# A fused Fourier layer and token FFN on one Trainium2 core: small products on the second stage's PSUM banks at planned places, the inverse second stage two steps later, C stored by quads, half of the threshold off VectorE

## Chip, core and metric

The kernel runs on one core of a Trainium2 chip. The metric is the device time in microseconds (us) of one execution. The kernel before takes 909.07 us, the median of 2 runs (907.66 to 910.48).

## The reference, cut to what matters

Eight batches of 3136 rows and 256 columns go through a real FFT along the rows, a complex 256x256 product per frequency, a bias, a soft threshold and the inverse FFT. Then 128 rows of each batch, those with the largest score, go through a small FFN and are written back.

```python
X = np.fft.rfft(x, axis=1)                      # x: 8 x 3136 x 256
Yr = Xr @ w_r - Xi @ w_i + b_r
Yi = Xr @ w_i + Xi @ w_r + b_i
Yr = np.sign(Yr) * np.maximum(np.abs(Yr) - lam, 0.0)   # the same for Yi
y = np.fft.irfft(Y, n=x.shape[1], axis=1)
...
scores = np.einsum('bsd,d->bs', y, w_gate)
top_idx = np.argpartition(-scores[b], capacity)[:capacity]   # capacity 128
h = np.maximum(xe @ w1, 0.0)
ye = h @ w2
out[b, top_idx] = y[b, top_idx] + g[:, None] * ye     # g = sigmoid(score)
```

## The kernel before

The FFT of 3136 points is done in two stages, 98 x 32, both as products with cosine and sine tables on TensorE (PE).

- **First stage** (`s1`, inverse `s1i`). A piece is 4 of the 32 columns n2 of a batch, so a batch has 8 pieces. GpSimd (POOL) forms sum and difference of the two halves (`uv_x`, lines 409 and 410; `uv_c`, lines 575 and 576; VectorE does the forward pair of batch 0 and the inverse difference of the last batch). Four products per piece go to two PSUM banks, ScalarE (ACT) copies them out (line 432 into `at`, line 584 into `ot`), and a DMA stores them: forward to the DRAM scratch `As`, inverse to the output.
- **Second stage, forward** (`s2`). A quad is a sixth of a batch's frequencies. It is loaded from `As` (tile `av`, two steps ahead), 32 small products fill the two banks of `px`, ACT casts `px` to the high part `Xh` (line 462) and VectorE (DVE) forms the low part `Xl` (line 463). `s2t` does the two odd frequencies of a batch in a bank of `s`.
- **Spectral product** (`spectral`). Per quad two halves p = 0 and 1, each 12 products of 512 columns (high x high, high x low, low x high) into one bank of `py`. `shrink` then does the threshold: DVE adds the bias in PSUM (line 479), ACT forms relu(z - 2 lam) into `r` (line 481), DVE forms min(z, 0) + r into `Y` (line 482). `spectral_t` does it for the odd frequencies.
- **Second stage, inverse** (`s2i`). 16 products into four banks of `s`. ACT copies each bank into `ct` (line 527), DVE forms the bank's part of the scores (`score_part`, line 509, name `junk`). Four DMAs per quad store `ct` into the DRAM scratch `Cs`, and `ld_c` loads a quarter of `Cs` as `cin` with one DMA.
- **Routing and FFN.** `score` transposes the score parts of a batch (`Csc`), multiplies them by `wq` and has the scores. `select` finds the 128th largest by a search over the bits of the float: per level DVE compares and counts (`f`, `c`, `n`, lines 269, 272, 277), PE sums the counts over partitions (`s<-n,tm`), DVE takes the digit (`ok`, `d`, `w`, lines 291 to 294). `place` turns the threshold into row numbers, `gather` fetches the rows, `prepare`, `hidden` and `combine` are the FFN. Batches 0 to 3 are selected together with 2 bits a level (16 levels), 4 and 5 together, 6 and 7 alone with 3 bits.

PSUM has 8 banks: `px` 2, `py` 2, and `s` 4. Everything but the forward second stage and the spectral products takes its bank from the ring `s`: both first stages, `s2i`, `s2t`, `s2it`, and every small product of routing and FFN.

The order of the work is written by hand. A step t is one quad; 48 steps make the main loop. In a step: all planned `s1` and `s1i` pieces (lists `F1` and `I1`), a turn of the routing threads, `s2` of quad t+1, `s2i` of quad t-1, the load of `av` for t+2, sums and differences, `spectral` half 0 with one turn of the threads in its middle, half 1 with another, then loads of `cin`. In steps 2 to 10 `consts_moe` loads a slice of the FFN weights and ACT rounds it (line 243). Threads are Python generators: a turn runs each one to its next `yield`, whatever the engines are doing. The engines execute their own instructions in the order in which the program issues them. All plain DMAs are issued by SyncE (SP, line 203). The matmuls all have line 206.

After the loop come the eight `s1i` pieces of batch 7, with one turn of the threads per piece, and then the rest of the routing and the FFN.

Of the kernel before, what the change touches and what calls it, by code (L numbers as in the profile page):

```python
# [20 lines left out]
N1, N2 = 98, 32  # L21
# [35 lines left out]
def _tables():  # L57
# [52 lines left out]
    gi = gi.reshape(6, 2, 128, 2, 2, 2, 16).transpose(2, 0, 1, 3, 5, 4, 6).reshape(128, NJ, 64)  # L110
# [3 lines left out]
    git = np.zeros((64, 2, 2, 16))  # L114
    for m, (r, k) in enumerate(fr):
# [45 lines left out]
def fourier_moe(ctx: ExitStack, tc: tile.TileContext, x, w_r, w_i, b_r, b_i, wg, w1, w2,  # L161
# [14 lines left out]
    second = c_tile([128, 2, NJ, 64], F32, "second")  # L176
# [19 lines left out]
    XB, CB = 3, 2  # L196
# [21 lines left out]
    def consts_w():  # L218
        for z, src in enumerate((w_r, w_i)):
# [3 lines left out]
            nc.vector.tensor_copy(h, t)  # L223
            nc.vector.tensor_tensor(out=l, in0=t, in1=h.bitcast(F32), op=ALU.subtract)
# [3 lines left out]
    def consts_bias():  # L228
# [24 lines left out]


    def select(bs, bits, thrs):
# [7 lines left out]
        for hi, i in zip([32] + cuts, cuts):  # L263
            m = 2 ** (hi - i) - 1
            f = pool.tile([N1, nb, m], U32, name="f" + tag, bufs=1)
            if w is None:
                nc.vector.memset(f, 0)
            else:
                nc.vector.tensor_tensor(out=f, in0=digits[:, 8 * i:8 * i + m].rearrange("p (o m) -> p o m", o=1).broadcast_to([N1, nb, m]),  # L269
                                        in1=w.broadcast_to([N1, nb, m]), op=ALU.bitwise_xor)  # L270
            c = pool.tile([N1, nb, m, N2], BF16, name="c_6" if nb == 1 else "c" + tag, bufs=1)
            nc.vector.tensor_tensor(out=c, in0=sv.broadcast_to([N1, nb, m, N2]),  # L272
# [3 lines left out]
            with nc.allow_low_precision(reason="counts up to 32 are exact"):  # L276
                nc.vector.tensor_reduce(out=n, in_=c, axis=AX.X, op=ALU.add)  # L277
            yield
            yield
            tot = ps.tile([N1, nb, m], F32, name="s", bufs=4)  # L280
            mm(tot, ones, n)
            w2 = pool.tile([N1, nb, 1], U32, name="w" + tag)
            if w is None:
                nc.vector.tensor_scalar(out=w2.bitcast(I32), in0=tot, scalar1=cap - 0.5, scalar2=1.0, op0=ALU.is_ge, op1=ALU.subtract)
            else:
                d = pool.tile([N1, nb, 1], U32, name="d" + tag, bufs=1)
                if m == 1:
                    nc.vector.tensor_scalar(out=d, in0=tot, scalar1=cap - 0.5, scalar2=None, op0=ALU.is_ge)
                else:
                    ok = pool.tile([N1, nb, m], F32, name="ok" + tag, bufs=1)  # L290
                    nc.vector.tensor_scalar(out=ok, in0=tot, scalar1=cap - 0.5, scalar2=None, op0=ALU.is_ge)  # L291
                    with nc.allow_low_precision(reason="whole numbers"):
                        nc.vector.tensor_reduce(out=d, in_=ok, axis=AX.X, op=ALU.add)  # L293
                nc.vector.scalar_tensor_tensor(out=w2, in0=d, scalar=i, in1=w, op0=ALU.logical_shift_left, op1=ALU.bitwise_xor)  # L294
# [4 lines left out]
    def place(b, thr, slots):  # L299
        m = pool.tile([N1, 2, N2], BF16, name="mask")  # L300
        nc.vector.tensor_scalar(out=m[:, 0, :], in0=scores[:, b, :], scalar1=thr, scalar2=None, op0=ALU.is_gt)
        nc.vector.tensor_scalar(out=m[:, 1, :], in0=scores[:, b, :], scalar1=thr, scalar2=None, op0=ALU.is_equal)
        mf = m.rearrange("p a c -> p (a c)")
        yield
        yield
        pt = ps.tile([2 * N2, N1], F32, name="s", bufs=4)
        mm(pt, mf, eye)
        mt = pool.tile([2 * N2, N1], BF16, name="mt")
        nc.vector.tensor_copy(mt, pt)
        yield  # L310
        yield
        pp = ps.tile([N1, 2, N2], F32, name="s", bufs=4)
        mm(pp.rearrange("p a c -> p (a c)"), mt, upper[:2 * N2, :])
        row = pool.tile([N1, 2, N2 + 2], F32, name="row")
        nc.vector.tensor_copy(row[:, :, :N2], pp)
        cnt = pool.tile([N1, 2], BF16, name="cnt")
        nc.vector.tensor_copy(cnt, pp[:, :, N2 - 1])
        for a in range(2):
            nc.vector.tensor_copy(row[:, a, N2 + 1:], nrow)
        yield  # L320
        yield
        pb = ps.tile([N1, 2], F32, name="s", bufs=4)
        mm(pb, lower, cnt, True, False)
        mm(pb[:, 1:2], ones, cnt[:, 0:1], False, True)
        nc.vector.tensor_copy(row[:, :, N2], pb)
        end = pool.tile([N1, 2], F32, name="end")
        nc.vector.tensor_tensor(out=end, in0=row[:, :, N2], in1=row[:, :, N2 - 1], op=ALU.add)  # L327
        for k in range(NCHK):
            n = min(128, cap - 128 * k)
            hot = pool.tile([N1, 2, n], F32, name="hot", bufs=1)  # L330
            io = iota[:N1, 128 * k:128 * k + n]
            for a in range(2):
                nc.vector.tensor_scalar(out=hot[:, a, :], in0=io, scalar1=row[:, a, N2:N2 + 1], scalar2=None, op0=ALU.is_ge)
                nc.vector.scalar_tensor_tensor(out=hot[:, a, :], in0=io, scalar=end[:, a:a + 1], in1=hot[:, a, :],  # L334
                                               op0=ALU.is_lt, op1=ALU.mult)
            yield
            yield
            pi = ps.tile([n, N2 + 2], F32, name="s", bufs=4)
# [3 lines left out]
            nc.vector.tensor_tensor(out=r, in0=tcol[:n, k:k + 1], in1=pi[:, N2:N2 + 1], op=ALU.subtract)  # L342
            le = pool.tile([n, N2], F32, name="le")
            c = pool.tile([n, 1], F32, name="col")
            nc.vector.tensor_scalar(out=le, in0=pi[:, :N2], scalar1=r, scalar2=None, op0=ALU.is_le)
            nc.vector.tensor_reduce(out=c, in_=le, axis=AX.X, op=ALU.add)
            idx = idxs[:n, NCHK * b + k:NCHK * b + k + 1]
            nc.vector.tensor_tensor(out=idx, in0=c, in1=pi[:, N2 + 1:], op=ALU.add)
# [460 lines left out]
```

## Time and profile before

| what | us |
|---|---|
| median of the runs | 909.07 |
| the profiled execution | 909.2 |
| its span, first to last instruction | 907.4 |
| around the span | 1.8 |
| first forward second stage (first step) starts at | 51.7 |
| that of the last quad starts at | 741.3 |
| last inverse second stage ends at | 786.7 |

Times in the rows are microseconds from the start of the span unless marked ns. A PE row's duration is modelled and overlaps with the next one's, so the pace of matmuls is read from their starts. "PEld" is PE's weight load. What stands behind "<-" is what ended an engine's idle time.

### The profile page before, as it was taken

To read this page: it belongs to the slowest core of one execution; us is meant where nothing else is said; L and a number is where in the kernel's file an instruction comes from. 1 tells how busy PE (TensorE), PEld (TensorE's weight loads), DVE (VectorE), ACT (ScalarE), POOL (GpSimd) and SP (SyncE) were. 2 spreads that over 40 slices of the span, in tenths; PEclk is the share of its full clock that TensorE was granted. 3 is DMA by queue.
4 is the path that set the end of the run, shared out by engine and by line. 5 is a ranking of instruction groups with operands and counts; after the bars stand their busy time and mean duration, and the time that the engine had idled before them with its cause. 6 is when DMAs were issued, how large, how long until landed. Compare 5 with 4: busy or idle time off the path is not lost. (4 is left out here: it accounts for less than half of the span.)

```text
span 907.4 us, 19138 instructions
## 1 busy us (share of the span) xinstructions
PE 723.9 (80%) x7618; PEld 476.0 (52%) x7618; DVE 444.8 (49%) x1244; ACT 333.1 (37%) x654; POOL 314.5 (35%) x266
## 2 busy tenths in 40 slices
PE   3369787767899899888797889898898978658775
PEld 1046555445666566555454555566566655422565
DVE  5225443332454354447655654655667765414652
ACT  2235243343455535553443444344233232202110
POOL 0233232436265536535441634344222132022101
PEclk9579898887999999998989999999899897855677
DMA  5787655766698779878765867675545433343100
GB/s 179 223 253 235 212 162 163 219 180 193 176 269 249 255 214 293 260 210 244 209 194 167 228 192 225 195 205 162 155 124 153 130 109 112 87 144 107 53 7 18
DMA packets 86995, 162.53 MB, mean 179 GB/s; under 512 B 8221, under 2 KB 60794, under 8 KB 86906
## 3 DMA queue, kind: packets, MB, share of 16 engines
q1 hardware_dynamic: 86010, 159.14, 59.8%
q0 software_dynamic: 896, 2.17, 0.8%
q8 instruction: 60, 0.98, 0.5%
q14 instruction: 29, 0.24, 0.1%
HBM read 83.22 MB, written 78.12 MB: 178 GB/s over the span
## 5 line engine op out<-in xcount | busy, mean ns | idle before, releaser
L206 PE MATMUL py<-wh,Xh 128*128 128x512 f32 x384 | 171.3, 446 | 2.4 <-issue 2.4
L481 ACT ACTIVATE r<-py,m2l 128x512 f32<-128x512 f32 (+1 forms) x104 | 69.8, 671 | 261.8 <-DVE py L479 259.7
L206 PE MATMUL py<-wl,Xh 128*128 128x512 f32 x384 | 159.1, 414 | 2.9 <-issue 2.9
L206 PE MATMUL py<-wh,Xl 128*128 128x512 f32 x384 | 159.8, 416 | 1.0 <-issue 1.0
L575 POOL TENSOR_TENSOR cu<-cin 113x512 f32<-113x512 f32 x64 | 82.1, 1283 | 190.1 <-DMA cin<-Cs 122.7
L463 DVE TENSOR_TENSOR Xl<-px,Xh 128x1024 fp32r<-128x1024 f32 x48 | 58.8, 1224 | 160.2 <-ACT Xh L462 160.1
L409 POOL TENSOR_TENSOR xu<-xt 113x512 f32<-113x512 f32 x56 | 71.9, 1284 | 173.2 <-PE s L206 172.3
L206 PE MATMUL s<-cu,first 49*64 49x512 f32 (+1 forms) x256 | 98.3, 692 | 37.9 <-POOL cu L575 16.9
L206 PE MATMUL s<-Y,second 32*64 32x256 f32 x1536 | 93.5, 449 | 42.2 <-DVE XTl L474 16.1
L509 DVE CUSTOM_DVE_ANT_0 junk<-s,wgb 128x256 f32<-128x256 f32 (+1 forms) x200 | 84.5, 422 | 44.8 <-PE s L206 21.7
L482 DVE SCALAR_TENSOR_TENSOR Y<-py,r 128x512 f32<-128x512 f32 x96 | 66.3, 691 | 78.3 <-ACT r L481 78.3
L527 ACT COPY ct<-s 128x256 f32<-128x256 f32 x192 | 66.8, 374 | 101.9 <-DVE Csc L509 61.7
L206 PEld LDWEIGHTS py<-wh,Xh 128*128 128x128 f32 x384 | 78.1, 203 | 47.7 <-issue 31.9
L206 PE MATMUL s<-xu,first 64*64 64x512 f32 (+1 forms) x256 | 73.1, 661 | 25.9 <-DVE xu L409 14.9
L206 PE MATMUL s<-cv,first 64*64 64x512 f32 (+1 forms) x256 | 87.9, 696 | 3.1 <-DVE cv L576 3.1
L479 DVE TENSOR_TENSOR py<-py,bias 128x512 f32<-128x512 f32 x96 | 66.7, 695 | 48.0 <-PE py L206 47.6
L206 PEld LDWEIGHTS py<-wl,Xh 128*128 128x128 f32 x384 | 77.4, 202 | 22.2 <-issue 3.3
L206 PEld LDWEIGHTS py<-wh,Xl 128*128 128x128 f32 x384 | 78.5, 205 | 17.2 <-issue 3.2
L584 ACT COPY ot<-s 113x512 f32<-113x512 f32 x128 | 67.9, 608 | 50.7 <-issue 28.7
L206 PEld LDWEIGHTS s<-Y,second 32*64 32x64 f32 x1536 | 43.3, 149 | 71.8 <-ACT ot L584 22.8
L206 PEld LDWEIGHTS px<-second,av 64*64 64x64 f32 x3072 | 62.6, 143 | 31.0 <-issue 14.8
L432 ACT COPY at<-s 113x512 f32<-113x512 f32 x128 | 66.0, 595 | 23.6 <-PE s L206 21.6
(109 smaller groups left out, 959.2 us busy)
## 6 DMA issues: line engine op xcount, KB each, us to landing
xt<-in_x SPq DMA_DIRECT2D x64, 392.0 KB
As<-at SPq DMA_DIRECT2D x64, 392.0 KB
cin<-Cs SPq DMA_DIRECT2D x32, 784.0 KB
out<-ot SPq DMA_DIRECT2D x64, 392.0 KB
av<-As SPq DMA_DIRECT2D x48, 512.0 KB
Cs<-ct SPq DMA_DIRECT2D x192, 128.0 KB
second<-t_second SPq DMA_DIRECT2D x2, 768.0 KB
w1s<-in_moe_w SPq DMA_DIRECT2D x1, 1024.0 KB
```

The costliest lines, as they stand in the source:

```text
L206: return nc.tensor.matmul(out, a, b, start=start, stop=stop)
L409: e.tensor_tensor(out=u, in0=t[:, 0, :], in1=t[:, 1, :], op=ALU.add)
L432: nc.scalar.copy(out=tv[:, r, :], in_=banks[r][:PT])
L463: nc.vector.tensor_tensor(out=lv, in0=p, in1=hv.bitcast(F32), op=ALU.subtract)
L479: nc.vector.tensor_tensor(out=p, in0=p, in1=bs, op=ALU.add)
L481: nc.scalar.activation(out=r1, in_=p, func=AF.Relu, bias=m2l[:p.shape[0]], scale=1.0)
L482: nc.vector.scalar_tensor_tensor(out=y, in0=p, scalar=0.0, in1=r1, op0=ALU.min, op1=ALU.add)
L509: nc.vector.tensor_tensor_reduce(out=junk[:r], in0=p, in1=wgb[:r], scale=1.0, scalar=0.0, op0=ALU.mult, op1=ALU.add, accum_out=Csc[b][:r, ...
L527: nc.scalar.copy(out=t[:, k], in_=banks[k])
L575: e.tensor_tensor(out=u, in0=t[:, 0, :], in1=t[:, 1, :], op=ALU.add)
L584: nc.scalar.copy(out=tv[:, r, :], in_=banks[r][:PT])
```

## The change

1. **Banks.** `px` becomes two tiles of one bank, `px0` and `px1`. The forward second stage fills both and empties each by itself. Every small product of routing and FFN, and the odd rows of the inverse (`s2it`), take them in turn (`m_tile`); `s2t` takes a `py` bank. Only `s1`, `s1i` and `s2i` are left in `s`.
2. **Places by running estimates.** Each matmul and each DVE instruction adds an estimate to a running clock of its engine while the program is written out. A thread yields the delay that it wants after its last DVE work, and a turn runs it only when PE's clock has reached that point. Turns are offered after every 3 spectral products (four in half 0, three in half 1).
3. **Later inverse.** `s2i` of quad t-2 instead of t-1 stands in step t; `s1i` begins at step 9 of a batch instead of 8.
4. **Threshold.** In half 1 DVE adds the bias into SBUF (`r0`); ACT then forms relu(z - 2 lam) and relu(-z), POOL subtracts the two. These three stand in the next step, behind `s2i`'s copies. Half 0 and the odd rows stay as they were.
5. **First-stage pieces.** One piece stands at the start of a step and the others between the two spectral halves.
6. **C.** `Cs` is laid out by quads: one store of 512 KB instead of four of 128 KB. A load of `cin` becomes three DMAs (48, 48 and 2 partitions).
7. **Rest.** Four buffers for `xt` (three before), three for `ct` (two); loads of `xt` ahead of the stores; the selection groups are (0,1), (2,3), (4,5), 6, 7; the score parts are issued in turns.

```diff
     def mm(out, a, b, start=True, stop=True):
+        k, m, n = b.shape[0], out.shape[0], int(np.prod(b.shape[1:]))
+        part = 8 if k <= 32 else 4 if k <= 64 and m <= 64 else 1
+        if part != clk["part"]:
+            clk["part"], clk["PE"] = part, clk["PE"] + 0.15
+        clk["PE"] += max(n * (1.68 if b.dtype == F32 else 0.45), 220 if b.dtype == F32 else 110) / part / 1000
         return nc.tensor.matmul(out, a, b, start=start, stop=stop)
+    class Vector:
...
+                clk["V"] = max(clk["V"], clk["PE"] + 0.2) + VB + n * VN
+                return f(*args, **kw)
+    def m_tile(shape):
+        turn[0] ^= 1
+        return ps.tile(shape, F32, name=f"px{turn[0]}", bufs=1)
...
-            yield
-            yield
-            tot = ps.tile([N1, nb, m], F32, name="s", bufs=4)
+            yield SL
+            tot = m_tile([N1, nb, m])
...
-        p = ps.tile([128, 2, 8, 64], F32, name="px", bufs=1)
+        p = [ps.tile([128, 8, 64], F32, name=f"px{kap}", bufs=1) for kap in range(2)]
...
-        nc.scalar.copy(out=hv, in_=p)
-        nc.vector.tensor_tensor(out=lv, in0=p, in1=hv.bitcast(F32), op=ALU.subtract)
+            for kap in range(2):
+                nc.scalar.copy(out=hv[:, kap], in_=p[kap])
+                vec.tensor_tensor(out=lv[:, kap], in0=p[kap], in1=hv[:, kap].bitcast(F32), op=ALU.subtract)
...
-        p = ps.tile([128, 2, 97], F32, name="s", bufs=4)
+        p = ps.tile([128, 2, 97], F32, name="py", bufs=2)
...
-        nc.vector.tensor_tensor(out=p, in0=p, in1=bs, op=ALU.add)
+        q = p if eng is vec else pool.tile(list(p.shape), F32, name="r0", bufs=2)
+        vec.tensor_tensor(out=q, in0=p, in1=bs, op=ALU.add)
...
+            def rest():
+                nc.scalar.activation(out=r1, in_=q, func=AF.Relu, bias=m2l[:p.shape[0]], scale=1.0)
+                nc.scalar.activation(out=q, in_=q, func=AF.Relu, scale=-1.0)
+                eng.tensor_tensor(out=y, in0=r1, in1=q, op=ALU.subtract)
+            shrinks.append(rest)
...
-        def store():
-            for p in range(2):
-                for half in range(2):
...
+        later.append(lambda: ld(Cs[b][0][g].rearrange("k p d -> p k d"), t))
...
-        ld(t[P0:], Cs[b][:, :, :, 4 * i:4 * i + 4, :].rearrange("p a r n d -> (a r) p n d"))
+        for a in range(2):
+            ld(t[16 + 48 * a:64 + 48 * a], c[a, :, :, 4 * i:4 * i + 4, :])
+        ld(t[P0::97], Cs[b][1].rearrange("(q a n) d -> a q n d", q=2, a=2)[:, :, 4 * i:4 * i + 4, :])
...
+    MID0, MID1, SL, FG, SC = (0, 1, 2, 3), (0, 1, 2), 0.15, 6.0, 4
-    I1 = [2, 3, 3, 4, 5, 5, 6, 6]
+    F1, I1 = [-2, -1, 0, 1, 1, 2, 3, 3], [9, 10, 10, 11, 12, 12, 13, 14]
...
+    def tick(most=None, wait=False):
+        score_some(SC)
+        most = MOST if most is None else most
+        for t in sorted(threads, key=lambda t: t[1]):
+            if most and (t[1] <= clk["PE"] or wait):
...
+            firsts = [(s1, a) for a in todo(t, "s1")] + [(s1i, a) for a in todo(t, "s1i")]
+            for f, a in firsts[:NQ]:
+                f(*a)
...
+                forward(t + 1)
+            inverse.append(t)
+            if t == T - 1:
+                flush(shrinks)
+            while inverse and inverse[0] <= t - (LAG if t < T - 1 else 1):
+                backward(inverse.pop(0))
+            flush(later)
+            flush(shrinks)
...
+            spectral(b, g, 0, tick)
+            last_rows()
...
+            for f, a in firsts[NQ:]:
+                f(*a)
...
+            spectral(b, g, 1, tick)
```

Three places show how it moves the instructions.

ACT in one step of the main loop, before: the two `r` are the threshold of the step's two halves, `at` and `ot` are the first-stage pieces of the next step, `Xh` and `ct` its second stages.

```order
L481 ACTIVATE r_3780<-py,m2l 128x512
L481 ACTIVATE r_3807<-py,m2l 128x512
L432 COPY at<-s 113x512 x4
L584 COPY ot<-s 113x512 x4
L462 CAST Xh<-px 128x2x8x64
L527 COPY ct<-s 128x256 x4
```

ACT in one step now (line numbers of the changed file):

```order
L461 COPY at<-s 113x512 x2
L502 CAST Xh<-px_3522 128x8x64
L502 CAST Xh<-px_3523 128x8x64
L584 COPY ct<-s 128x256 x4
L528 ACTIVATE r_3506<-r_3504,m2l 128x512
L529 ACTIVATE r_3504<-r_3504 128x512
L524 ACTIVATE r_3639<-py,m2l 128x512
L633 COPY ot<-s 113x512 x2
```

The threshold of half 1 (the pair of lines 528 and 529) has moved behind the next step's copies and reads SBUF; only one `r` per step still reads a `py` bank in the step itself.

PE in half 0 of a step with selection, before: `py` is the spectral product, `n` the counts of one level.

```order
L206 MATMUL s<-Y,second 64x256 x16
L206 MATMUL py<-wh,Xh 128x512
L206 MATMUL py<-wh,Xl 128x512
L206 MATMUL py<-wl,Xh 128x512
L206 MATMUL py<-wh,Xh 128x512
L206 MATMUL py<-wh,Xl 128x512
L206 MATMUL py<-wl,Xh 128x512
L206 LDWEIGHTS tm
L206 MATMUL s<-n_4676,tm 98x12
```

PE in half 1 of such a step now:

```order
L216 MATMUL s<-cu,first 64x512
L216 MATMUL s<-cv,first 64x512
L216 MATMUL py<-wh,Xh 128x512
L216 MATMUL py<-wh,Xl 128x512
L216 MATMUL py<-wl,Xh 128x512
L216 LDWEIGHTS tm
L216 MATMUL px_3289<-n_3237,tm 98x6
L216 MATMUL py<-wh,Xh 128x512
```

The small product stands behind 3 spectral products instead of 6, writes a `px` bank, and has a first-stage piece in front of the half.

DVE behind the last inverse second stage, before: `Csc` is the last score part of batch 7, `cv` the difference of a loaded piece, `ok` to `n` one level of selection, `sct` the score transpose.

```order
L509 ISA junk,Csc<-s,wgb 64x256
L509 ISA Csc 64x1
L576 TENSOR_TENSOR cv<-cin_90 113x512
L291 TENSOR_SCALAR ok_8713<-s 98x7
L293 TENSOR_REDUCE d_8712<-ok_8713 98x1
L294 SCALAR_TENSOR_TENSOR w_8711<-d_8712,w_8555 98x1
L269 TENSOR_TENSOR f_8717<-digits,w_8711 98x7
L272 TENSOR_TENSOR c_8719<-scores,f_8717 98x224
L277 TENSOR_REDUCE n_8721<-c_8719 98x7
L576 TENSOR_TENSOR cv<-cin_90 113x512
L309 CAST mt<-s 64x98
L556 COPY sct<-s 25x128
```

The same place now, with two row searches (`row`, `end`, `hot`) between what is shown and `sct`:

```order
L230 ISA Csc 128x1
L230 TENSOR_TENSOR cv<-cin_91 113x512 x2
L230 TENSOR_SCALAR ok_9045<-px_9041 98x7
L230 TENSOR_REDUCE d_9044<-ok_9045 98x1
L230 SCALAR_TENSOR_TENSOR w_9043<-d_9044,w_8922 98x1
L230 TENSOR_TENSOR f_9049<-digits,w_9043 98x7
L230 TENSOR_TENSOR c_9051<-scores,f_9049 98x224
L230 TENSOR_REDUCE n_9053<-c_9051 98x7
L230 COPY row<-px_9055 98x2
L230 TENSOR_TENSOR end<-row 98x2
```

Both differences still stand ahead of the selection and of `sct`, but the transpose and the score product are now in PE's order ahead of all eight pieces of batch 7, not among them.

## Rows read from the trace of the kernel before

**Rows 1.** The page's first part: busy us, share of the span, instructions.

```profile
PE 723.9 (80%) x7618; PEld 476.0 (52%) x7618; DVE 444.8 (49%) x1244; ACT 333.1 (37%) x654; POOL 314.5 (35%) x266
```

**Rows 2.** Windows: length, busy us per engine, granted clock, DMA share, GB/s, by stage.

```profile
0.00:51.70 51.70, 15.89 (x68) 4.85 (x68) 19.12 (x28) 12.10 (x21) 5.12 (x8) 0.73 0.63 200
51.70:741.30 689.60, 593.32 (x6878) 396.14 (x6882) 352.51 (x960) 291.15 (x571) 280.49 (x234) 0.93 0.70 203
741.30:786.70 45.40, 37.81 (x311) 23.72 (x304) 26.89 (x84) 15.03 (x32) 10.23 (x9) 0.85 0.30 86
786.70:907.40 120.70, 76.93 (x370) 51.28 (x368) 46.32 (x173) 14.81 (x30) 18.70 (x16) 0.65 0.23 68
```

**Rows 3.** Waits in the main loop, 51.7 to 741.3: us in total, times, longest.

```profile
ACT r L481 <- DVE py L479: 238.4, 97, 5.4
...
PE s L206 <- ACT at L432: 36.1, 26, 6.0
...
ACT w2h L243 <- DMA xe<-in_moe_w: 26.3, 8, 5.5
...
PE s L206 <- ACT ct L527: 18.6, 17, 2.1
```

**Rows 4.** Timeline at 464 to 466 us, ACT, then PE: start, us, what, idle before.

```profile
464.65 0.69 ACT L481 ACTIVATE r<-py,m2l 128x512 f32<-128x512 f32 x1 [3.28 <-DVE py L479]
465.24 2.04 ACT L432 COPY at<-s 113x512 f32<-113x512 f32 x4
465.96 0.61 PE L206 MATMUL s<-cu,first 64*64 64x512 f32 x1 [1.74 <-ACT at L432]
```

**Rows 5.** Timeline of PE at 405 to 409 us, one step without a wait.

```profile
405.84 1.16 PE L206 MATMUL px<-second,av 64*64 64x64 f32 x64
406.94 1.12 PE L206 MATMUL s<-Y,second 32*64 32x256 f32 x32
407.99 0.50 PE L206 MATMUL py<-wh,Xh 128*128 128x512 f32 x1
408.32 0.39 PE L206 MATMUL py<-wh,Xl 128*128 128x512 f32 x1
408.55 0.39 PE L206 MATMUL py<-wl,Xh 128*128 128x512 f32 x1
```

**Rows 6.** Groups by line over the span: busy us, mean ns, idle before.

```profile
L481 ACT ACTIVATE r<-py,m2l 128x512 f32<-128x512 f32 (+1 forms) x104 | 69.8, 671 | 261.8 <-DVE py L479 259.7 <-DMA xt<-in_x 2.1
L482 DVE SCALAR_TENSOR_TENSOR Y<-py,r 128x512 f32<-128x512 f32 x96 | 66.3, 691 | 78.3 <-ACT r L481 78.3
...
L410 POOL TENSOR_TENSOR xv<-xt 113x512 f32<-113x512 f32 x56 | 72.1, 1288 | 0.0
L509 DVE CUSTOM_DVE_ANT_0 junk<-s,wgb 128x256 f32<-128x256 f32 (+1 forms) x200 | 84.5, 422 | 44.8 <-PE s L206 21.7 <-ACT ct L527 1.6 <-ACT ctt L543 0.2
```

**Rows 7.** One selection level on DVE in the timeline at 772 us, first and last of six.

```profile
772.01 0.16 DVE L291 TENSOR_SCALAR ok<-s 98x7 f32<-98x7 f32 x1
...
773.22 0.39 DVE L277 TENSOR_REDUCE n<-c 98x7 bf16<-98x224 bf16 x1
```

**Rows 8.** Tile `mask` on DVE: duration ns min/median/max.

```profile
L301 DVE TENSOR_SCALAR mask<-scores,w x8: 232/241/2997, 544.7 to 877.4; 98x32 bf16<-98x32 f32 x8
```

**Rows 9.** Timeline behind the loop: SP, DVE and PE.

```profile
792.45 0.79 SPq L203 DMA_DIRECT2D cin<-Cs  x2
798.77 0.69 DVE L576 TENSOR_TENSOR cv<-cin 113x512 f32<-113x512 f32 x1 [10.49 <-DMA cin<-Cs]
807.21 0.41 PE L554 MATMUL s<-ident,Csc 128*25 128x128 f32 x1
823.15 1.20 PE L206 MATMUL s<-sct,wq 25*98 25x32 f32 x6
882.39 0.23 PE L206 MATMUL s<-tm,mask 98*64 98x98 bf16 x1
```

**Rows 10.** Window of the densest stretch, columns as in rows 2.

```profile
335.00:438.00 103.00, 91.75 (x1145) 59.95 (x1151) 52.40 (x126) 50.46 (x101) 54.37 (x44) 0.97 0.83 248
```

More of the change, by code (lines that the diff above doesn't have):

```diff
@@ L413, in uv_x @@
         if n < 8 * B:
-            later.append(lambda: ld_x(*divmod(n, 8)))
+            loads.append(lambda: ld_x(*divmod(n, 8)))
     def quarters(z, uv):
@@ L423, in quarters, with evict @@
         return banks
+    count = [0]
+    def evict(tv, banks):
+        count[0] += 1
+        for r in range(2):
+            if r == 1 and count[0] % EV[1] < EV[0]:
+                vec.tensor_copy(tv[:, r, :], banks[r][:PT])
+            else:
+                nc.scalar.copy(out=tv[:, r, :], in_=banks[r][:PT])
     def s1(b, i):
@@ L430, in s1 @@
         tv = t.rearrange("p (r c) d -> p r (c d)", r=2)
-        for r in range(2):
-            nc.scalar.copy(out=tv[:, r, :], in_=banks[r][:PT])
+        evict(tv, banks)
         later.append(lambda: ld(As[b][:, 4 * i:4 * i + 4, :], t[P0:]))
@@ L685, in quad, with forward, backward, last_rows @@
         return divmod(t, Q)
+    loads, inverse, tails = [], [], []
+    def forward(n):
+        b, g = quad(n)
+        s2(b, g)
+        if g == Q - 1:
+            s2t(b)
+    def backward(n):
+        score_some(9)
+        b, g = quad(n)
+        s2i(b, g)
+        if g == Q - 1:
+            tails.append(b)
+    def last_rows():
+        if tails:
+            s2it(tails[0])
+            score_some(9)
+            done["s2i"] = tails.pop()
+            flush(later)
+    def load_a(n):
+        b, g = quad(n)
+        ld_a(b, g)
+        if g == Q - 1:
+            ld_at(b)
+    def sums(t):
+        for f, what, made, n in ((uv_x, "uvx", xuv, 2), (uv_c, "uvc", cuv, 2)):
+            for s in (t - 1, t):
+                while todo(s, what) and len(made) < n:
+                    a = todo(s, what)[0]
+                    f(*a)
+                    plan[s].remove((what, a))
     with tc.manual_schedule():
         for t in xts + cts:
-            nc.vector.memset(t[:P0].rearrange("p a c -> p (a c)") if len(t.shape) == 3 else t[:P0].rearrange("p a c d -> p (a c d)"), 0.0)
+            vec.memset(t[:P0].rearrange("p a c -> p (a c)") if len(t.shape) == 3 else t[:P0].rearrange("p a c d -> p (a c d)"), 0.0)
         ld(first.rearrange("p z c s -> p (z c s)"), t_first)
@@ new lines, in fourier_moe @@
+        sums(-1)
+        flush(loads)
+        forward(0)
+        ld(sec[:, 1].rearrange("p j s -> p (j s)"), t_second[:, NJ * 64:])
+        for t in range(T):
+            if t + 2 < T:
+                load_a(t + 2)
+            for a in todo(t, "ldc"):
+                ld_c(*a)
+            flush(loads)
+            firsts = [(s1, a) for a in todo(t, "s1")] + [(s1i, a) for a in todo(t, "s1i")]
+            for f, a in firsts[:NQ]:
+                f(*a)
+                sums(t - 1)
+            score_some(9)
+            if t + 1 < T:
+                forward(t + 1)
[4 more added lines that the diff above has]
+                backward(inverse.pop(0))
+            flush(later)
+            flush(shrinks)
@@ L754, in fourier_moe @@
-            tick(threads)
-            spectral(b, g, 1, mid)
+                sums(t - 1)
+            flush(later)
+            sums(t)
+            spectral(b, g, 1, tick)
             X.pop((b, g))
```

385 lines of the change are left out of this document (190 added, 195 removed).

## Prediction

> **What bounds the kernel now.** I read the page's busy shares first, then the span cut into stages, then what ended the waits in the longest stage, then the timeline at one such wait.
>
> TensorE is busy 80% of the span [rows 1]; ACT, DVE and POOL are far from full. The reader is to see that no engine is a bound by itself and that the order of the work costs the rest. By stage [rows 2]: 51.7 us until the first step, 689.6 us of main loop (47 steps, 14.67 us each), 45.4 us for what follows the last forward second stage, and 120.7 us behind the last inverse second stage. In the loop PE is idle 689.6 - 593.3 = 96.3 us, and its granted clock is 0.93 of the full 2.4 GHz. I read that as 7% of the 593.3 us lost to the lower level, 41.5 us. So the loop's work at the full clock is 552 us, 11.7 us a step, and 138 us are lost. A step without a wait bears that out [rows 5]: 1.10 us for the forward second stage and 1.05 for the inverse one (from start to next start), 0.23 us for each of 24 spectral products (5.5 us), together 7.7; first-stage pieces, odd rows, selection and FFN are the other 4.0.
>
> What ends PE's idle time in the loop is mostly ACT [rows 3]: 36.1 us for `at`, 18.6 us for `ct`. The cause is one row higher: ACT sat 238.4 us in front of `r`, waiting for DVE's bias addition. ACT works in order, so the copies that free PE's banks stand behind an `r` that is not ready. The timeline shows one such place [rows 4]: `r` starts at 464.65 after 3.28 us of waiting, `at` follows at 465.24, and PE, which wants the bank, has stood 1.74 us at 465.96. A smaller part is the rounding of the FFN weights: ACT waits 26.3 us for 8 slices [rows 3].
>
> Behind the loop the bound is a chain of small operations: the C piece lands and DVE takes it at 798.77; the scores of batch 7 are transposed at 807.21, 20.5 us after they could be, because pieces of `s1i` stand in front; the score product starts at 823.15; the search ends with the mask at 882.39; 25.0 us of row search, gather and FFN end the span at 907.4 [rows 9].
>
> **The change, part by part.** The sum is made against the profiled execution, 909.2 us with 1.8 us around its span, which is 0.1 us from the median.
>
> *Main loop.* Of the two `r` of a step one moves behind the next step's copies, where its addition is long done; the other stands before the pieces of the middle, whose banks are wanted only about 3 us later. `s2i` two steps late never waits for a fresh `Y`, and with only three users left in `s`, small products no longer queue for a bank behind a copy. `s2t` and `s2it` leave `s` too. So I take the waits on `at`, `ct` and the odd rows as gone. What is late next:
> - `s2i` needs the two banks of the piece at the step's start. ACT needs two copies for them, about 1.3 us at the 0.67 of line 481, the nearest of that width [rows 6]; PE arrives after the 1.10 us of the forward stage. About 0.25 us a step, 47 times: 12 us.
> - The first small product wants a `px` half after 1.10 + 1.05 + 0.8 = 2.95 us. The half is free after 1.10 + two casts of 0.67 + one DVE pass of 0.69 = 3.1 us plus hand-over. About 0.3 us a step: 14 us.
> - The FFN weight slices are still rounded on ACT in the first steps; their loads now have less in front of them on SP. I keep half of 26.3: 13 us.
> - One selection level takes DVE 1.6 us [rows 7]; with two levels, four score parts (0.42 each), two additions, one final threshold pass and two `Xl` halves (five passes of the 0.69 of line 482) DVE has about 8.4 us in a step [rows 6]. That fits into 12, with small slips: 5 us.
>
> That is 552 + 12 + 14 + 13 + 5 = 596 us, 12.7 us a step, 94 less than now. Covers: ACT gets 47 more passes of 0.67 (32 us), 54% of 596; DVE loses 47 of its 0.69 us passes; POOL gets 47 subtractions. The trace has no POOL subtraction of 128x512. The nearest row is line 410, 113x512 at 1.29 us [rows 6]; I take that, with 0 and twice it as ends. POOL then has 280 + 61 = 341 us in 596, and `Y` of half 1 is not needed for a whole step, so it is hidden at either end. The store of a quad in one DMA and the load in three move the same bytes; no row shows such a transfer, I bound it by 1 us a step either way and take 0, since nothing on PE waits for it directly. One more `xt` buffer and the earlier loads are hidden as the present ones are. The first 51.7 us stay: nothing in the change touches the loads that PE waits for there; 3 us either way.
>
> At the selection the Trainium skill has a rule against this change: the page SBUF — State Buffer, section "SBUF: two separate sides", says that DVE and GpSimd share one pair of ports as an exclusive lock, held for a whole instruction when the DVE operation has two SBUF inputs or runs in a two-port mode. The trace agrees in part: one `mask` pass takes 241 ns in the median and 2997 at most [rows 8], about two POOL operations more. By that rule alone, with each of the 56 levels in the loop held up by one POOL operation of 1.29 us and PE behind it, the whole would be 849; by the row such a hold-up is rare, and it lies inside the 5 us above.
>
> *Last quads (45.4 us).* PE's 37.8 busy us at clock 0.85 are 32 us of work. New on the path is the last threshold over POOL, 0.69 + 2 x 0.67 + 1.29 = 3.3 us, of which the odd rows' products hide about 1.4. I take 34.
>
> *Behind the last inverse (120.7 us).* The transpose moves ahead of the pieces, but DVE's copy of it still stands behind two differences that wait for the C load. The load lands about 11 us after the last inverse (now 12.1, with fewer stores ahead on SP). Then come 1.4 us of differences, about 8 us of DVE work (two levels at 1.6, two row searches, the copies) and some 3.5 us of hand-overs to PE and back: the scores stand at 24 us, now at about 38. From there DVE's queue holds 17 levels (counted in the order of instructions: 12 of batch 7 and 5 of batch 6), 27 us, six more differences, 4 us, and about 4 us of FFN passes; with 10 us of waits for PE the mask comes at 69 us, now at 95.7. The last 25.0 us stay. Together 94.
>
> *Sum.* 51.7 + 596 + 34 + 94 = 775.7 us of span, 777 us with the 1.8.
>
> **Rivals.**
> - *The transfers become the bound of the loop.* Now they take 0.70 of the DMA engines at 203 GB/s [rows 2]. The same bytes in 596 us are 235 GB/s and a share of 0.81. For: the late loads of `cin` now sit in front of `Y` on POOL. Against: 103 us of this kernel ran at 0.83 and 248 GB/s with PE busy for 91.75 of them [rows 10]. If the share stays at 0.75, the loop takes 0.70 x 689.6 / 0.75 = 644 us, the whole 825.
> - *The loop's loss stays and changes its name*, from ACT's order to DVE's. For: DVE's queue gains the level chains between the halves. Against: half of the additions no longer hold ACT. Then 51.7 + 690 + 34 + 94 + 1.8 = 871, faster only by the tail.
> - *PE stands behind its small products.* This one ends on the other side. PE has 106 rows of small products before the last inverse second stage, each in its in-order queue, most of them after 3 spectral products (0.7 us) instead of 6, at places from estimates that do not know when DVE waits for ACT. If each stops PE for a whole level of DVE, 1.6 us [rows 7], that is 170 us: 947. It is slower than before by 2% from 1.4 us each. The 2997 ns pass shows that a DVE operation can take 2.7 us more than its median [rows 8]. Against: a turn is skipped until the estimated time has come, and there are 2 us of spectral products plus a piece between most pairs.
> - *Better than forecast*: nothing is left over in the loop (560) and the tail's waits vanish (84): about 730. It lies at the low end.
>
> **How the numbers follow.** Forecast, between 728 and 824: 0.68. Transfers, 825 to 860: 0.15. Loss stays, about 870: 0.06. Small products, slower: 0.05. Below 728: 0.06. The forecast's own ends are about 730 from the better case and 824 from the unknown C transfers at their upper end, 1 us in each of 47 steps. The range takes in the transfer case: 728 to 860. About 2% is what a measurement of this kernel tells from no change. All cases but the small products end below 891, which is 2% faster: 0.95, of which I give 0.03 to mixtures that end within 2%. So 0.92 faster, 0.03 within, 0.05 slower.
>
> **What would show it.** Right: a distance of 12 to 13 us between forward second stages through the loop; the waits of PE on `at` and `ct` below 25 us together; the granted clock of the loop above 0.96; the score product of batch 7 within 25 us of the last inverse; a span's end 90 to 100 us behind it. The transfers' rival shows as a DMA share near 0.75 with POOL waiting for `cin` and PE for POOL; the third as PE waits on DVE `n`, `cnt` or `hot` of more than 100 us. The forecast is wrong if the steps stay above 14 us, or if a new wait on POOL's `Y` in front of `s2i` shows up.

## The result and the profile after

The kernel after the change takes 856.0 us (median of 2 runs, 852.92 to 859.08) against 909.07: a ratio of 0.9416, 95% interval 0.9258 to 0.9575. It is faster, and inside the range; the forecast was 777.0, a gain of 132 us where 53 were measured. The profiled execution has a span of 857.3 us.

The page's first part and the stages (length, busy us of PE, PEld, DVE, ACT and POOL, granted clock, DMA share, GB/s), the answer to [rows 1, 2]:

```profile
PE 706.8 (82%) x7635; PEld 456.8 (53%) x7635; DVE 521.8 (61%) x1344; ACT 354.4 (41%) x750; POOL 377.9 (44%) x314
```

```profile
0.00:50.60 50.60, 14.24 (x67) 4.29 (x68) 19.95 (x29) 12.20 (x21) 5.13 (x8) 0.77 0.64 212
50.60:705.60 655.00, 590.18 (x6911) 386.53 (x6915) 418.40 (x1026) 310.01 (x660) 338.46 (x279) 0.94 0.75 210
705.60:753.20 47.60, 39.91 (x317) 21.37 (x310) 24.50 (x85) 17.80 (x41) 13.71 (x11) 0.75 0.47 123
753.20:857.30 104.10, 62.44 (x352) 44.65 (x352) 58.90 (x205) 14.42 (x30) 20.59 (x16) 0.70 0.31 78
```

The main loop took 655.0 us where 596 were forecast: 59 of the 81.6 us by which the span missed its 775.7. The last quads missed by 13.6, the end by 10.1, the start came 1.1 earlier. PE's work is the forecast one (590.2 us at 0.94 are 555 at the full clock, 552 forecast); the losses are not: 65 us idle and 35 at the lower level. And DVE, which lost 48 threshold passes, is busy 77 us longer than before. A part of that is more work: with smaller selection groups there are 75 levels, before 58.

Waits in the loop, 50.6 to 705.6, answering [rows 3]:

```profile
POOL Y L530 <- ACT r L529: 241.4, 41, 18.8
...
PE px L216 <- DVE n L230: 29.6, 19, 4.6
...
ACT w2h L270 <- DMA xe<-in_moe_w: 28.8, 7, 6.4
...
PE s L216 <- ACT at L461: 12.6, 5, 3.0
```

PE's 54.7 us for `at` and `ct` are 12.6 now, below the 25 that were named as the sign. New at the top of PE's list is `n`, the last DVE operation of a selection level (4.5 us before), and POOL now stands 241 us in front of `Y`. The groups that grew, first of before, then of after (busy us, mean ns):

```profile
L272 DVE TENSOR_TENSOR c<-scores,f 98x224 bf16<-98x224 f32 (+5 forms) x58 | 26.2, 451 | 2.0
...
L269 DVE TENSOR_TENSOR f<-digits,w 98x7 uint32<-98x7 uint32 (+5 forms) x54 | 13.1, 242 | 1.9
L294 DVE SCALAR_TENSOR_TENSOR w<-d,w 98x1 uint32<-98x1 uint32 (+2 forms) x54 | 12.7, 236 | 1.9
```

```profile
L230 DVE TENSOR_TENSOR c<-scores,f 98x192 bf16<-98x192 f32 (+3 forms) x75 | 61.7, 823 | 2.6
L230 DVE TENSOR_TENSOR f<-digits,w 98x6 uint32<-98x6 uint32 (+2 forms) x70 | 44.2, 632 | 2.4
L230 DVE SCALAR_TENSOR_TENSOR w<-d,w 98x2 uint32<-98x2 uint32 (+1 forms) x70 | 35.0, 500 | 2.4
...
L230 DVE TENSOR_REDUCE n<-c 98x6 bf16<-98x192 bf16 (+3 forms) x75 | 25.7, 343 | 2.6
```

These means mix sizes. At one size, before and after:

```profile
L272 DVE TENSOR_TENSOR c<-scores,f 98x192 bf16<-98x192 f32 x15 | 5.4, 358 | 0.5
L269 DVE TENSOR_TENSOR f<-digits,w 98x6 uint32<-98x6 uint32 x15 | 2.5, 166 | 0.5
```

```profile
L230 DVE TENSOR_TENSOR c<-scores,f 98x192 bf16<-98x192 f32 x45 | 45.3, 1006 | 1.5
L230 DVE TENSOR_TENSOR f<-digits,w 98x6 uint32<-98x6 uint32 x45 | 36.1, 802 | 1.5
```

`w` of 98x2 went from 217 to 570 ns. `w`, `f` and `c` read two tensors in SBUF and take 2.6 to 4.8 times as long at these sizes; at those of batches 6 and 7, which are selected alone, `f` and `c` did not grow (`f` of 98x7 211 ns, before 218; `c` of 98x224 392, before 442). `n`, with one tensor, is as it was (353 ns at 98x192 in both), and so is the score part `junk<-s,wgb`, with one of its two in PSUM (423 ns, before 422). What the slow ones lie beside shows in the timeline at 501 us, DVE, then POOL, then PE (start, us, what, idle before):

```profile
501.94 0.84 DVE L230 SCALAR_TENSOR_TENSOR w<-d,w 98x2 uint32<-98x2 uint32 x1
502.81 1.20 DVE L230 TENSOR_TENSOR f<-digits,w 98x6 uint32<-98x6 uint32 x1
504.04 1.40 DVE L230 TENSOR_TENSOR c<-scores,f 98x192 bf16<-98x192 f32 x1
505.48 0.35 DVE L230 TENSOR_REDUCE n<-c 98x6 bf16<-98x192 bf16 x1
```

```profile
501.47 1.29 POOL L530 TENSOR_TENSOR Y<-r,r 128x512 f32<-128x512 f32 x1 [8.10 <-ACT r L529]
502.72 1.27 POOL L437 TENSOR_TENSOR xu<-xt 113x512 f32<-113x512 f32 x1
503.94 1.28 POOL L438 TENSOR_TENSOR xv<-xt 113x512 f32<-113x512 f32 x1
```

```profile
505.88 0.17 PE L216 MATMUL px<-n,tm 98*98 98x6 bf16 x1 [1.08 <-DVE n L230]
```

POOL waited 8.10 us for `r` and then ran `Y` and the sums queued behind it without a gap. `w` ends 0.02 us behind `Y`, `f` 0.02 behind `xu`, `c` 0.22 behind `xv`: three operations of one level each gave way to one POOL operation, and PE stood at the counts. Of all `c`, `f`, `w`, `mask`, `hot` and the gate's `junk`, 11 of 222 took over 0.9 us before, 82 of 271 after (counted over the traces). All 93 began while a POOL operation ran and ended 0.01 to 0.42 us behind the end of one. Of those that began while POOL was idle, 182 before and 148 after, none took over 0.1 us more than the shortest of its kind and size. 40 before and 123 after began beside POOL; the time held, over that shortest one, is 16 us before and 106 after.

### The profile page after: what moved, and what is told of

Same layout as the page of the kernel before. It is cut to its first block, busy times and chain, and to the rows that moved or that the text cites. A ratio compares the mean times of both kernels' runs of the same rounds, so it can differ in the third digit from the quotient of the medians.

```text
span 857.3 us, 19356 instructions
## 1 busy us (share of the span) xinstructions
PE 706.8 (82%) x7635; PEld 456.8 (53%) x7635; DVE 521.8 (61%) x1344; ACT 354.4 (41%) x750; POOL 377.9 (44%) x314
## 4 chain that ended last, share of the span: by engine, by line
PE 44%; DVE 25%; DMA 13%; ACT 8%; issue 7%; POOL 1%; SPq 1%; POOLq 0%; DVEq 0%; ACTq 0%
PE py L216 21%; PE s L216 15%; PE px L216 9%; DVE c L230 5%; DVE junk L230 4%; DVE f L230 4%; DVE w L230 3%; DMA As<-at 2%; DVE Xl L230 2%; DMA xe<-in_moe_w 2%; ACT at L461 2%; DMA cin<-Cs 2%; ACT ct L584 1%; DVE n L230 1%; DMA Cs<-ct 1%
## 5 line engine op out<-in xcount | busy, mean ns | idle before, releaser
L530 POOL TENSOR_TENSOR Y<-r,r 128x512 f32<-128x512 f32 x48 | 61.6, 1283 | 282.4 <-ACT r L529 258.6
L524 ACT ACTIVATE r<-py,m2l 128x512 f32<-128x512 f32 (+1 forms) x56 | 36.8, 657 | 208.1 <-DVE py L230 208.1
L230 DVE TENSOR_TENSOR Xl<-px,Xh 128x512 fp32r<-128x512 f32 x96 | 61.8, 686 | 99.4 <-ACT Xh L502 99.4
L623 POOL TENSOR_TENSOR cu<-cin 113x512 f32<-113x512 f32 x64 | 84.7, 1325 | 47.9 <-DMA cin<-Cs 18.9
L216 PE MATMUL s<-xu,first 49*64 49x512 f32 (+1 forms) x256 | 83.2, 677 | 26.8 <-DVE xu L230 12.1
L230 DVE CUSTOM_DVE_ANT_0 junk<-s,wgb 128x256 f32<-128x256 f32 x192 | 81.2, 423 | 28.5 <-ACT ct L584 7.6
L216 PE MATMUL s<-Y,second 32*64 32x256 f32 x1536 | 81.3, 418 | 17.9 <-ACT at L461 12.6
L216 PE MATMUL s<-cu,first 49*64 49x512 f32 (+1 forms) x256 | 81.8, 680 | 3.1 <-POOL cu L623 2.9
L216 PEld LDWEIGHTS py<-wh,Xl 128*128 128x128 f32 x384 | 77.9, 203 | 10.5
L216 PE MATMUL s<-xv,first 64*64 64x512 f32 (+1 forms) x256 | 77.2, 677 | 0.0
L216 PE MATMUL s<-cv,first 64*64 64x512 f32 (+1 forms) x256 | 75.1, 680 | 0.3 <-POOL cv L625 0.2
L625 POOL TENSOR_TENSOR cv<-cin 113x512 f32<-113x512 f32 x56 | 72.5, 1294 | 0.0
L438 POOL TENSOR_TENSOR xv<-xt 113x512 f32<-113x512 f32 x56 | 72.1, 1287 | 0.0
```

The lines of the kernel that those rows point to most:

```text
L230: return f(*args, **kw)
L438: e.tensor_tensor(out=v, in0=t[:, 0, :], in1=t[:, 1, :], op=ALU.subtract)
L524: nc.scalar.activation(out=r1, in_=q, func=AF.Relu, bias=m2l[:p.shape[0]], scale=1.0)
L530: eng.tensor_tensor(out=y, in0=r1, in1=q, op=ALU.subtract)
L623: nc.gpsimd.tensor_tensor(out=u, in0=t[:, 0, :], in1=t[:, 1, :], op=ALU.add)
L625: e.tensor_tensor(out=v, in0=t[:, 0, :], in1=t[:, 1, :], op=ALU.subtract)
```

## Experiments

The theory after this: a DVE operation with two SBUF inputs waits until the POOL operation beside it ends (called the lock here), and PE waits behind it. Rivals: the number and the places of the levels in the queues (order), and the transfers, at 0.75 of the DMA engines. Every ratio below is to the kernel before, measured beside it.

**1. The same queues, one SBUF input.** The kernel leaves out the search: the three operations of a level become reductions, and rows are picked by a threshold that means nothing.

```diff
-vec.tensor_tensor(out=f, in0=digits[...], in1=w..., op=ALU.bitwise_xor)
+vec.tensor_reduce(out=f, in_=digits[...], axis=AX.X, op=ALU.add)
...
-vec.tensor_tensor(out=c, in0=sv..., in1=f..., op=ALU.is_ge)
+vec.tensor_reduce(out=c, in_=wgb[...], axis=AX.X, op=ALU.add)
...
-vec.scalar_tensor_tensor(out=w2, in0=d, scalar=i, in1=w, ...)
+vec.tensor_reduce(out=w2, in_=d, axis=AX.X, op=ALU.add)
```

> Left out: the search of the threshold. The three operations f, c and w of a level become reductions of the same sizes with one SBUF input, at the same places in every queue; POOL's work and all transfers stay. Lock theory (a DVE operation with two SBUF inputs stands until POOL's queue has a gap, and PE behind it): f near 160 ns, c 350 to 400, w near 160 in the mean (now 632, 823, 500), DVE busy 522 to about 430 us, main loop 655 to 595-615 us, the whole 795 to 820. Order theory (the number and the places of the levels hold PE, whatever a level takes): main loop 645 to 660, the whole 845 to 860. Transfer theory (0.75 of the DMA engines is the bound): 845 to 860.

790.5 us, ratio 0.8705 (0.8641 to 0.877). The three groups and the loop's window:

```profile
L230 DVE TENSOR_REDUCE c<-wgb 98x192 bf16<-98x192 f32 (+3 forms) x75 | 25.0, 333 | 0.0
...
L230 DVE TENSOR_REDUCE w<-d 98x2 uint32<-98x2 uint32 (+1 forms) x70 | 10.8, 155 | 2.4
L230 DVE TENSOR_REDUCE f<-digits 98x6 uint32<-98x6 uint32 (+2 forms) x70 | 10.5, 149 | 0.0
```

```profile
51.20:647.70 596.50, 569.31 (x6907) 377.12 (x6911) 329.14 (x1028) 310.33 (x660) 335.93 (x279) 0.97 0.81 231
```

Same order, same levels, same bytes, same POOL work: the loop takes 596.5 us, the forecast's 596, and PE's wait on `n` is gone from it. Order falls, and so do the transfers: they ran at a share of 0.81 and 231 GB/s, where the forecast had 0.81 and 235.

**2. POOL's differences left out** (`v = u` for `x` of batches 1 to 7 and C of batches 0 to 6).

> Left out: the differences on POOL (the sum is used in their place), 112 operations of 1.26 us, POOL busy 378 to about 237 us; DVE's and PE's instructions stay. Lock theory: the bursts on POOL are half as long, the 105 us by which f, c, w and their like are stretched fall below 45, the whole 800 to 830. Order theory and transfer theory: f, c and w stay within a fifth of 632, 823 and 500 ns or it makes no difference that they shrink, the whole 843 to 858.

805.4 us, ratio 0.8878 (0.8829 to 0.8926). `f`, `c` and `w` fell to 490, 616 and 463 ns, less than expected, and the time held from 106 to 70 us where below 45 was expected; yet the time fell by 51 us, as expected. The loss follows POOL's operations, but 36 us less held do not by themselves give 51: what the 112 missing operations gave back in another way is not separated here.

**3, 4. The deferral undone; POOL's subtraction behind the sums.**

```diff
-    YP, EV = (1,), (0, 2)
+    YP, EV = (), (0, 2)
```

```diff
-                eng.tensor_tensor(out=y, in0=r1, in1=q, op=ALU.subtract)
+                subs.append(lambda: eng.tensor_tensor(out=y, ...))
...
             sums(t)
+            flush(subs)
             spectral(b, g, 1, tick)
```

> The deferred threshold of half 1 undone: both halves add the bias in PSUM, ACT's r stands in the step, DVE ends both; POOL loses 48 subtractions, 61 us. If the deferral is what freed ACT's order, at and ct come back in PE's waits (36 and 18.6 us before) and the whole is 880 to 905. If the lock costs more than the deferral gives: f, c and w fall to about 250, 450 and 240 ns as before, DVE gets 33 us more of final passes, the whole 825 to 850. Order theory with neither: 850 to 865.

> POOL's subtraction stands behind the sums of the step in its queue, no longer in front of them; no work added or removed. Burst theory (POOL sits 241 us before Y waiting for ACT's r, and the sums then run back to back and shut DVE out): f, c, w fall at least by a third, the whole 820 to 842. Lock theory without bursts (the share of time in which POOL works decides): f, c and w stay, the whole 850 to 860. Order theory: 850 to 860; slower, up to 880, if s2i then waits for Y.

830.6 us, ratio 0.9133 (0.9065 to 0.9202), and 827.6 us, 0.9111 (0.9051 to 0.9171): both faster than the change by 25 us or more. Without the deferral `f`, `c` and `w` fall to 285, 582 and 344 ns, and ACT waits for `r` again, 322.7 us over the span. Yet PE's wait for `at` in the loop is this, and `ct` is not in its list:

```profile
PE s L216 <- ACT at L461: 21.2, 14, 3.1
```

That is 21 us of the 54.7 before, against 12.6 with the deferral: most of this gain came from the rest of the change (banks, places, the later inverse), not from the deferral. In the fourth run POOL's work is all there, only its order differs (groups of POOL and DVE):

```profile
L530 POOL TENSOR_TENSOR Y<-r,r 128x512 f32<-128x512 f32 x48 | 61.5, 1282 | 29.5 <-issue 23.0 <-ACT r L529 6.5
```

```profile
L230 DVE TENSOR_TENSOR c<-scores,f 98x192 bf16<-98x192 f32 (+3 forms) x75 | 42.7, 569 | 2.6
...
L230 DVE SCALAR_TENSOR_TENSOR w<-d,w 98x2 uint32<-98x2 uint32 (+1 forms) x70 | 27.0, 385 | 2.4
...
L230 DVE TENSOR_TENSOR f<-digits,w 98x6 uint32<-98x6 uint32 (+2 forms) x70 | 23.8, 340 | 2.4
```

POOL hardly waits for `r` (6.5 us), operations over 0.9 us fall from 82 to 36, and the time held from 106 to 57 us. POOL's runs without a gap are hardly shorter (3.3 operations in the mean, 3.7 in the change, counted over the traces), but 63 of the 271 operations begin beside POOL, not 123: what moved is where the runs lie.

**5, 6. The subtraction on DVE; more work on POOL.**

```diff
-                eng.tensor_tensor(out=y, in0=r1, in1=q, op=ALU.subtract)
+                vec.tensor_tensor(out=y, in0=r1, in1=q, op=ALU.subtract)
```

```diff
             sums(t)
+            ex = pool.tile([128, 2, D], F32, name="ex", bufs=1)
+            nc.gpsimd.tensor_tensor(out=ex, in0=bias, in1=bias, op=ALU.add)
             spectral(b, g, 1, tick)
```

> The deferred subtraction stays where it is in the program but runs on DVE, not on POOL: POOL loses 61 us and its waits for r, DVE gains 48 operations of about 0.69 us with two SBUF inputs. Lock with bursts: f, c and w fall as in the run with the late subtraction (340, 569, 385 ns or less), the new operation itself is stretched now and then, the whole 820 to 845. If what helped there and in the run without the deferral was something else than POOL's queue: 850 to 870.

> Added: one POOL addition of 128x512 in each step behind the sums, with a result that nobody reads, some 60 us of POOL; nothing else moves. Lock theory: it lengthens bursts, f, c and w grow by a tenth or more (now 632, 823, 500 ns), the whole 864 to 885. Order and transfer theories: POOL has 0.56 of the span free, the whole 850 to 861.

Both missed. The fifth took 889.4 us, ratio 0.9827 (0.977 to 0.9884): `f`, `c` and `w` fell (402, 460, 408 ns), but DVE, in order, now waits for ACT itself, 82.5 us, and PE waits 25.5 us for banks that the score parts hold:

```profile
DVE Y L230 <- ACT r L529: 82.5, 48, 2.5
```

```profile
PE s L216 <- DVE Csc L230: 25.5, 25, 5.4
```

The sixth took 851.4 us, ratio 0.9364 (0.9281 to 0.9446), no slower than the change, with 50.7 us more POOL work. That lies where order and transfers were expected to leave it; it does not speak for the lock, and run 1 is what rules those two out. `c` grew by a tenth (906 ns), `f` did not (639). Counted over the trace, only 12.5 of the 50.7 us lie over an operation that took more than 0.9 us, and the time held is 109 us, in the change 106. POOL's total is not the price.

**7, 8. `d`, `w` and `f` in the PSUM bank of the level's counts**, alone and with the late subtraction.

```diff
+                f = tot[:, 32:32 + nb * m].bitcast(U32)...
...
-                                        in1=w.broadcast_to(...), op=ALU.bitwise_xor)
+                                        in1=wp.broadcast_to(...), op=ALU.bitwise_xor)
...
+            if wp is not None:
+                w = pool.tile([N1, nb, 1], U32, name="w" + tag)
+                vec.tensor_copy(w, wp)
...
+                w2 = tot[:, 24:24 + nb].bitcast(U32)...
...
-                d = pool.tile([N1, nb, 1], U32, name="d" + tag, bufs=1)
+                d = tot[:, 16:16 + nb].bitcast(U32)...
```

> d, w and f of a level lie in the PSUM bank of its counts, so that w, f and c have one SBUF input and one in PSUM; a copy of w to SBUF (0.15 us) is added behind n, off the way to PE; POOL as it is now. Lock by the number of SBUF inputs: f and w 160 to 230 ns, c 390 to 450, the whole 790 to 820, near the 790 of the run without a search. If any SBUF input beside POOL is locked out, or the write to SBUF: f, c and w stay above 450, the whole 850 to 870. If the longer hold of the px bank stops the forward second stage: 825 to 845 with new waits of PE on DVE for px.

> The same with POOL's subtraction behind the sums. If the lock is gone from the search, the order on POOL is worth little more: 5 to 15 us less than the kernel with PSUM alone, by the row and FFN operations that still have two SBUF inputs (junk, hot, mask): 780 to 810. If bursts matter for another reason, 25 us less, as between the late subtraction and the kernel after.

810.2 us, ratio 0.8924 (0.8868 to 0.8981). The kernel leaves nothing out, and the search is no longer shut out. `c` still reads one SBUF tensor and writes SBUF, so neither of these alone is what holds it. PE's wait on a level in the loop is 8.2 us, in the change 29.6. `mask` and `junk`, which read SBUF as before, still are:

```profile
L230 DVE TENSOR_TENSOR c<-scores,px 98x192 bf16<-98x192 f32 (+2 forms) x70 | 24.7, 352 | 2.4
L230 DVE CUSTOM_DVE_ANT_0 junk<-xe,wgb 128x256 f32<-128x256 f32 x8 | 19.2, 2399 | 0.0
L230 DVE TENSOR_SCALAR mask<-scores,w 98x32 bf16<-98x32 f32 x16 | 13.2, 884 | 0.1
L230 DVE TENSOR_TENSOR px<-digits,px 98x6 uint32<-98x6 uint32 (+2 forms) x70 | 11.8, 169 | 2.4
```

The eighth took 827.0 us, ratio 0.9097 (0.9018 to 0.9175), slower than the seventh, where 5 to 15 us less were expected: with the lock out of the search, the late subtraction is left with its price, PE's wait in front of `s2i` (3.1 us in the seventh):

```profile
PE s L216 <- POOL Y L541: 17.2, 13, 3.2
```

It is also no faster than the fourth (827.6), which has the same late subtraction and 57 us held where this one has 17. There the search's lock cost nothing that can be measured. That fits time held on DVE being paid only where PE stands behind it, which no run tested by itself.

**9, 10. LAG = 1 beside run 3; the deferral undone beside run 7.**

```diff
-    AVB, CTB, OTB, LAG = 2, 3, 3, 2
+    AVB, CTB, OTB, LAG = 2, 3, 3, 1
```

> Beside the run without the deferral: the inverse second stage of a quad one step later, as before the change, not two. If the two steps are what keeps s2i from waiting for a fresh Y: PE gets waits on Y in front of s2i of about 1 us a step, 40 to 60 us in all, the whole 865 to 895. If the banks and the order of ACT are enough and half 1 of the quad before is ended by the time the forward stage is through: 825 to 840, within the interval of the run without the deferral (830.6). The lock theory says nothing here; f, c and w as there (285, 582, 344 ns) within a fifth.

> f, d and w in PSUM, and the deferral undone. If the deferral's only cost was the lock, it is worth having once the lock is gone, since ACT's order gains by it: 815 to 835, slower than the 810 of PSUM with the deferral. If POOL's subtraction costs in another way too (junk at 2399 and mask at 884 ns are still shut out): 785 to 805. Order theory as such: no forecast.

834.0 us, ratio 0.9175 (0.9104 to 0.9247), and 813.9 us, 0.8948 (0.8874 to 0.9022): each within the interval of the run that it is compared with. The later inverse, tried without the deferral, and the deferral, tried without the lock in the search, give nothing that can be measured.

**11, 12. The gate's sum on PE, beside run 7; then the last batch's first two `cv` on POOL.**

```diff
-        vec.tensor_tensor_reduce(out=junk, in0=xe, in1=wgb[:n], ..., accum_out=sg)
...
+                pg = m_tile([n, 1])
+                for h in range(2):
+                    mm(pg, xT[:, h, :], wgc[:, h:h + 1], h == 0, h == 1)
+                nc.scalar.activation(out=ga, in_=pg, func=AF.Sigmoid)
```

```diff
-        e = vec if b == B - 1 else nc.gpsimd
+        e = vec if b == B - 1 and i > 1 else nc.gpsimd
```

> With f, d and w in PSUM, the gate's sum (junk from xe and the gate's weights, two SBUF inputs, 8 times 2399 ns, 19.2 us) leaves DVE for two small products per slice on PE. Lock theory: DVE loses 19 us, of which PE stood behind a part; the whole 797 to 808. If these stretches lie where nobody waits: 808 to 813, the same within the interval.

> Beside the run with the gate on PE: the first two differences of the last batch go to POOL, so that DVE's queue no longer stands in front of them until the C load lands, 13.6 us in which PE stands behind a small product of the selection. If that wait holds the chain of the end: what follows the last inverse second stage shrinks from about 112 us by 6 to 10, the whole 787 to 792. If the chain stands behind the C load anyway (the pieces and the scores of batch 7 wait for it too): 794 to 801, no difference. Slower, 800 to 806, if the two further POOL operations shut out what is left with two SBUF inputs (hot, mask).

797.3 us, ratio 0.8789 (0.8689 to 0.8889), and 790.4 us, 0.875 (0.8694 to 0.8807). The first interval still touches run 7's (0.8868 to 0.8981). Between the two the longest wait of PE on a level (named by `w`, whose copy is now its last operation) went from 13.6 to 3.7 us (the last number of the rows, run 11, then run 12):

```profile
PE px L217 <- DVE w L231: 25.9, 13, 13.6
```

```profile
PE px L217 <- DVE w L231: 15.1, 12, 3.7
```

From the last inverse second stage to the end it is 106 us, from 113. These intervals overlap too, so each step by itself is indicated by medians and traces, not settled; both together are (run 12's interval ends at 0.8807, run 7's begins at 0.8868). Run 12 beats both kernels, by about 66 us the change.

## Why the prediction was wrong

- **The failed step** is the fourth term of the loop, "with small slips: 5 us", and behind it the reading that by the row a hold-up of DVE by POOL is rare. Run 1 puts the search's lock at 655.0 - 596.5 = 58.5 us in the loop, and at 857.3 - 788.1 = 69.2 over the whole. The median of `mask` [rows 8] was taken as an odds; it only tells how seldom POOL happened to work beside it before. Of all such operations 40 of 222 began beside POOL then, 123 of 271 after. And the cover that `Y` on POOL is "hidden at either end" priced how long `Y` takes, not that it waits: POOL stood 241 us in front of it with the sums behind, and with the subtraction behind the sums (run 4) only 63 began beside POOL.
- The Trainium skill's rule, page SBUF — State Buffer, section "SBUF: two separate sides", was weighed and set aside; the runs agree with it. Its 849 us came near the 856 partly by luck: one hold-up was priced for each of 56 levels in the loop, where the trace has 51; the timeline shows up to three in a level; and of 106 us held, about 69 were paid (run 1). The Trainium skill, same page, section "Who interferes with whom", says that a DVE operation with at most one SBUF input, outside the two-port modes, does not contend with GpSimd; runs 1 and 7 agree (`f` at 149 and 169 ns, not 632).
- **Right: the rest of the loop.** 552 us of work, 596 without the lock, the DMA share. The split of the other 39 us was not, so it is in part luck that 596 fits so closely: in run 1 PE idles 27 us, of which 10.4 is `at`, and 17 us are the clock at 0.97, which had no term. The waits of `s2i` and for a `px` half, 26 us in the sum, hardly show.
- **ACT's order, half right.** The waits on `at` and `ct` went as said. But the deferral, to which the text gave this, removed the smaller part of them (run 3). ACT's wait for the FFN slices did not halve (28.8, was 26.3).
- **The last quads**, 34: 47.6. It was 42.2 in run 1 but 47.9 in run 7, so how much of it is the lock is not shown. The text took PE's work there at the full clock, and the granted one was 0.75; it left out `s2i` waiting for score parts, 4.5 us in run 1; the wait for `Y` over POOL was 3.1 (1.9 forecast).
- **The end**, 94: 104.1, and 98.2 in run 1. The score product started 20.5 us behind the last inverse (the scores were forecast at 24); it was the search after it that took longer: the mask's product came at 77.9 us, forecast at 69, and at 72.0 in run 1.
- **Rivals.** The transfers (825 to 860, chance 0.15) held the 856 by number and showed a part of their sign, a share of 0.75, but fell with run 1, where the share rose to 0.81. "The loop's loss stays and changes its name" (871, chance 0.06) named DVE and was the nearest in mechanism; its reason, the longer queue, was not the cause. Slow small products, PE waiting a whole level each, did not come: 29.6 us on `n`.
- **Small slips of the working**, which decide nothing: 775.7 + 1.8 is 777.5, 2997 - 241 ns is 2.8 us, and 18 levels, not 17, lie behind the last inverse.

## What to carry to other kernels

When work moves to GpSimd, ask which VectorE operations with two SBUF inputs will lie beside it: look for pairs that end together in the timeline, and price one GpSimd operation for each that begins beside one, whatever the median of a time with few neighbours says. When an engine is made to wait, what is queued behind it moves with it; what mattered here is where that work then lay, not its total (runs 4 and 6). A small operand that comes out of PSUM anyway can stay there: in run 7 its chain was no longer held.

## What was not expected of the hardware

The hold-up is mostly one POOL operation, but 3 of the 271 operations took 3.08, 5.76 and 6.18 us. One of them, DVE, then POOL:

```profile
441.41 5.76 DVE L230 TENSOR_TENSOR c<-scores,f 98x192 bf16<-98x192 f32 x1
```

```profile
440.99 1.00 POOL L422 DMA_INDIRECT out<-ye,idxs  x1 [2.72 <-DVE d L230]
442.02 1.29 POOL L437 TENSOR_TENSOR xu<-xt 113x512 f32<-113x512 f32 x1
443.25 1.27 POOL L438 TENSOR_TENSOR xv<-xt 113x512 f32<-113x512 f32 x1
444.47 1.26 POOL L623 TENSOR_TENSOR cu<-cin 113x512 f32<-113x512 f32 x1
445.69 1.26 POOL L625 TENSOR_TENSOR cv<-cin 113x512 f32<-113x512 f32 x1
```

`c` began before `xu`, beside the issue of an indirect DMA, and ended only behind `cv`: four operations passed it. The Trainium skill, page SBUF — State Buffer, section "SBUF: two separate sides", has the pair held for one whole instruction; that alone does not account for four. All three lie just behind or across such an issue, and it recurs: in runs 2, 3, 4, 6 and 9 the longest `c` that began beside the issue took 3.33, 8.18, 9.40, 6.75 and 10.62 us. But the 2997 ns `mask` before, passed by two, began 2.0 us behind one, and a `junk` of run 4 (5.76 us) 3.2 us; what decides it stays open. `mask`, one SBUF tensor and a column of scalars, is held too: 2 of 16 before (3.00 and 1.78 us, against 0.24), 4 of 16 after (1.22 to 1.32).
